# An attention and mixture-of-experts kernel: filler matmuls with a named bank, the expert loop's blocks in another order, and table reads taken ahead on ScalarE

## The chip, the cores and the metric

The kernel runs on one core of one Trainium2 chip. The metric is the device time of one execution, in microseconds (us). The kernel before took 606.84 us (median of three runs: 606.8, 606.84 and 608.63). The profile was taken in an execution of its own, which took 614.04 us.

## The reference

An attention without a score matrix feeds a layer of experts of which each token uses one.

```python
# q, k, v: 8 batches, 8 heads, 576 rows, 64 columns
q_s = softmax(q, axis=-1)                 # over the 64 columns
k_s = softmax(k, axis=2)                  # over the 576 rows
kv  = einsum('bhsd,bhse->bhde', k_s, v)   # 64 x 64 for each head
x   = einsum('bhsd,bhde->bhse', q_s, kv)  # turned to 4608 tokens x 512

logits = x @ w_gate                       # 8 experts
expert_idx = argmax(logits, axis=1)       # one expert for each token
gate_w = softmax(logits)[token, expert_idx]
for e in range(8):                        # tokens sorted by expert
    h = relu(x_sorted[lo:hi] @ w1[e])     # 512 -> 1024
    y_sorted[lo:hi] = h @ w2[e]           # 1024 -> 512
out = gate_w[:, None] * unsort(y_sorted)
```

## The kernel before

**Two stages.** The attention, the gate and the sorting of the tokens take about the first 199 us; they are straight code without a branch. Then comes a loop over blocks of tokens whose number and widths are known only at run time, since they depend on how many tokens went to each expert.

**The attention's order is written out by hand.** The string ORDER is a list of 804 words such as `TR.4.0.21`. A word names a step (TR), its batch (4) and its part (0). `Plan.emit` walks the list and lets each step issue its instructions on all the engines that it uses. So the place of a word in the list is the place of its instructions in the queue of each engine. Steps that matter below: KM0 to KM4 take the maximum of k, KS subtracts it, KE applies the exponential; QS and QE do the like for q; TR transposes a group of q (qT, L531, with the copy qTs by ScalarE, L536); KV forms the product of k and v (a matmul that sets the bank to a start value, L416, and the products, L427); G0, G2 transpose and gate with it (kvT, L451; kg, L460); MM multiplies q with kv (xp, L543 and L546); R0 to R9 and RB, RC, RD, RG rank the tokens of each expert (rk, L611 to L615, read on VectorE at L627).

**Fills.** A fourth number in a word is a count of fills: matmuls of a constant, 128 columns by 384, whose result nobody reads. They stand on TensorE ahead of the step's own instructions, in places where TensorE would sit idle, and keep it active. There are 215 of them, all issued at L220. A fill needs a PSUM bank to write to. `fill` asks `spots.oldest`, which looks at the live buffers of the pools tr, xp and sm and takes the one whose readers were issued longest ago; if there is none it takes the bank `hot`. The pool kv is not looked at. A fill that writes to a bank waits until the bank's readers are done, as every write does.

**The loop over blocks.** Each engine runs its own copy of a loop at run time, and the engines meet by semaphores. A table in SBUF (`tab`) holds a row of numbers for each pass: KD is the kind of the block, LW says that a new expert's weights begin. Kind 12 is a block of 3 x 128 tokens, 11, 10 and 9 are narrower by 32 tokens at a time, 3 to 8 have 2 x 128 tokens, and below 3 the block is tiny. TensorE's `body` reads the kind and branches: one of six pieces of code for layer 1 (`layer1`, 96 matmuls with their weight loads, L1009; or `tiny1`), and then layer 2, up to three times 24 matmuls (`layer2`, L1025, or `half`, L1067). The six pieces stand in the code one behind the other: tiny, 2 x 128, 288, 320, 352, and last 3 x 128. Behind them stands layer 2. In this case the passes have the kinds 12 (five times), 11, 8, 10, 8, 10, 8, 9, 8 and 2.

**The work around the loop's start.** Before the loop, TensorE finishes a layer 2 of the first block (L1107) and transposes the tokens of the next (L1123); ScalarE copies these to xh (L1154), VectorE makes the remainder xl (L1245), and the first layer 1 of the loop waits for xl. In the loop, ScalarE makes the high part of the hidden layer (`relus`, L1170) and VectorE the low part (L1259). VectorE's transposition of the next tokens (L1236) stands between the third and the fourth of the eight low parts, and waits for the loads xt and gx. ScalarE's `body` reads three numbers of the table at the start of a pass (kind, fresh, turn) and one more after the relus.

Of the kernel before, what the change touches and what calls it, by code (L numbers as in the profile page):

```python
# [37 lines left out]
LK.0.0 LK.0.1 LK.0.2 LV.0.0 LK.1.0 LK.1.1 LV.0.1 LV.0.2 LQ.0.0 LK.2.0 CD.0.0 LK.2.1 LV.1.0 LV.1.1 LV.1.2 KM0.0.0 KM0.0.1 KM1.0.0  # L38
KM2.0.0.24 KM3.0.0 KM4.0.0.4 KR.0.0 KS.0.1 KS.0.2 KS.0.0 KM0.1.0 KS.0.3 KM0.1.1 KM1.1.0 ER.0.0 KE.0.0 KE.0.2 KE.0.1 KE.0.3
KV.0.0.24 KM2.1.0.1 KV.0.1.1 KV.0.2.1 KV.0.3 KM3.1.0 N0.0.0 N1.0.0 QM.0.0 N2.0.0 G0.0.0.11 QS.0.0 G1.0.0 QE.0.0 QE.0.1 KM4.1.0  # L40
G2.0.0.16 TR.0.0 QS.0.1 KS.1.3 KS.1.2 KR.1.0 KS.1.0 KM0.2.0 KS.1.1 KM0.2.1 CS.0.0 KM1.2.0 QE.0.2 KE.1.3 ER.1.0 G3.0.0 QE.0.3
EX.0.0 TR.0.1.2 MM.0.0.1 TR.0.2 KE.1.2 KE.1.1 EX.0.1 EX.0.2 KE.1.0 KM2.2.0.1 TR.0.3 MM.0.1 KV.1.0 KV.1.1 KV.1.2.1 KV.1.3 LQ.1.0
WG.0.0 LQ.0.1 WG.0.1 LV.2.0 LQ.1.1 LV.2.1 LV.2.2 LK.3.0 LK.3.1 LV.3.0 WG.0.2 DE.0.0 RE.0.0 KM3.2.0 EV.0.0 DE.0.1 QM.1.0 RE.0.1
N0.1.0 N1.1.0 EV.0.1 WH.0.0 EX.0.3 N2.1.0 KM4.2.0 MM.0.2 MM.0.3.4 G0.1.0 KS.2.0 KS.2.3 DE.0.2 KR.2.0 QMR.1.0 KS.2.2 KS.2.1
RE.0.2 EV.0.2 DE.0.3 RE.0.3 EV.0.3 LS.0.0 QS.1.0 QS.1.1 QSR.1.0 WL.0.0 QE.1.0 KE.2.3 ER.2.0 QE.1.1 QE.1.2 KE.2.1 G1.1.0 WH.0.1
# [12 lines left out]
KM2.5.0 KV.4.1 KV.4.2 TR.3.4 MM.3.2 KV.4.3 KM0.6.0 R8.2.0 KM3.5.0 R6.1.0 RE.3.1 EV.3.1 KM0.6.1 N0.4.0 R1.2.0 DE.3.2 R3.2.0
N1.4.0 RE.3.2 R4.2.0 EV.3.2 QM.4.0 EX.3.4 N2.4.0 R9.2.0 MM.3.3 MM.3.4.3 KM4.5.0 R5.2.0 G0.4.0 RC.2.0 KS.5.1 DE.3.3 RG.2.0 KS.5.3
KR.5.0 KS.5.2 RB.2.0 RD.2.0 R6.2.0 KS.5.0 RE.3.3 KM1.6.0 EV.3.3 DE.3.4 PU.1.4 WL.0.3 WL.0.4 QS.4.0 QS.4.1 RH.2.0 PU.2.1 PU.2.0  # L60
TR.4.0.21 QE.4.0 ER.5.0 QE.4.1 G1.4.0 EX.4.0 TR.4.1 KM2.6.0.1 G2.4.0.1 RE.3.4 KM3.6.0 EV.3.4 LS.3.0 R0.3.0 R8.3.0 R1.3.0 R3.3.0
R4.3.0 QE.4.2 QE.4.3 KE.5.3 G3.4.0 KE.5.0 EX.4.1 KE.5.1 KE.5.2 R9.3.0 LQ.5.0 LQ.4.1 LV.6.0 LV.6.1 LV.6.2 LQ.5.1 WG.0.6 WG.0.7
LK.7.1 KV.5.0.3 MM.4.0 KM4.6.0 KV.5.1 KV.5.2 TR.4.2 R5.3.0 KV.5.3 MM.4.1 KR.6.0 DE.4.0 KS.6.2 KM0.7.0 RE.4.0 KS.6.1 RB.3.0
N0.5.0 RD.3.0 EV.4.0 RC.3.0 KS.6.0 N1.5.0 DE.4.1 RG.3.0 KS.6.3 R6.3.0 RE.4.1 QM.5.0 KM0.7.1 EV.4.1 QMR.5.0 KE.6.1 ER.6.0 N2.5.0
KE.6.0 WH.0.5 EX.4.2 KE.6.2 G0.5.0.17 TR.4.3.4 EX.4.3 G1.5.0 PU.2.3 RH.3.0 PU.2.2 PU.3.0 PU.3.2 QS.5.0 QSR.5.0 QS.5.1 KV.6.0
MM.4.2 KV.6.1 TR.5.0 MM.4.3 G2.5.0 KV.6.2 TR.5.1.1 QE.5.0 QE.5.1 QE.5.2 QE.5.3 KE.6.3 G3.5.0 WH.0.6 WH.0.7 EX.5.0 EX.5.1 LQ.6.0
LV.7.0 DE.4.2 RE.4.2 EV.4.2 DE.4.3 RE.4.3 KM1.7.0 EV.4.3 KV.6.3.1 MM.5.0 TR.5.2 MM.5.1 TR.5.3 EX.5.2 EX.5.3 LS.4.0 R0.4.0 N0.6.0
DE.5.0 N1.6.0 RE.5.0 R8.4.0 R1.4.0 EV.5.0 R3.4.0 R4.4.0 DE.5.1 QM.6.0 RE.5.1 TR.5.4 KM2.7.0 MM.5.2 R5.4.0 N2.6.0 R9.4.0 EX.5.4
PU.3.1 PU.3.3 PU.3.4 WL.0.6 RH.4.0 WL.0.5 WL.0.7 QS.6.0 QS.6.1 EV.5.1 KM3.7.0 DE.5.2 R6.4.0 RB.4.0 RE.5.2 RD.4.0 EV.5.2 G0.6.0.3
# [12 lines left out]
RB.7.3 VL.7.1 RD.7.3 L3.3.5 RH.7.3 RH.6.0 PU.6.2 PU.6.1 PU.6.0 RH.7.0 PU.6.3 PU.7.2 PU.7.4 PU.7.3 PU.7.1 PU.7.0 T3.7.0 L1.3.7
L1.3.6 L2.3.7 L2.3.6 T5.7.0 T6.7.0 L3.3.7 L3.3.6 T7.7.0 T8.7.0 L4.3.0 T9.7.0
# [5 lines left out]
class Spots:  # L89
    def __init__(self):  # L90
        self.last, self.of, self.count = {}, {}, 0

    def tile(self, pool, shape, *a, tag, **k):
        t = pool.tile(shape, *a, tag=tag, **k)
        if len(shape) == 3 and shape[1] == 2:
            self.last[tag] = t[:, 0, :HOT]
        elif len(shape) == 3 and shape[1] * shape[2] == 512:
            self.last[tag] = t[:, :HOT // shape[2], :]
        else:
            self.last[tag] = t[:, 512 - HOT:] if shape[1] == 512 and tag == "sm" else None  # L100
        return t

    def taken(self, tag, until, bufs):
        if tag in ("tr", "xp", "sm"):
            self.of[tag] = (self.of.get(tag, []) + [(self.last.get(tag), until)])[-bufs:]

    def oldest(self, when):
        best = None
        for tiles in self.of.values():
            for t, until in tiles:  # L110
                n = [when(a) for a in until]
                if t is not None and n and None not in n and (best is None or max(n) < best[0]):
                    best = max(n), t
        return best and best[1]


class Plan:
# [7 lines left out]
    def emit(self, order, fill):  # L125
# [5 lines left out]
        for key, word in zip(queue, words):  # L131
# [10 lines left out]
            if x.take:  # L142
                self.spots.taken(x.take, x.until, self.bufs[x.take])
# [804 lines left out]
def experts(nc, tc, g):  # L948
# [46 lines left out]
    def pe():  # L995
# [470 lines left out]
```

## Time and profile before

| what | value |
|---|---|
| median of three runs | 606.84 us |
| the profiled execution | 614.04 us |
| its span in the trace | 612.3 us |
| TensorE busy | 579.6 us, 95% of the span |
| VectorE busy | 315.4 us, 52% |
| ScalarE busy | 234.8 us, 38% |
| GpSimd busy | 131.0 us, 21% |
| loop's first matmul | at 217.83 us of the span |

The span runs from the first to the last instruction in the trace. The profiled execution was 7.2 us slower than the median of the runs. "PE" is TensorE, "PEld" its weight loads, "DVE" VectorE, "ACT" ScalarE, "POOL" GpSimd and "SP" the queue of SyncE, which here issues loads. A number in brackets at the end of a row is the time for which the engine had been idle, and the name behind the arrow is what ended that; "issue" means that the engine waited for nothing that the profile shows. [...]

### The profile page before, as it was taken

The page shows a single profiled execution, that of the slowest core. Times are in us where ns is not written, and L with a number is a line of the kernel's source. Part 1 is how long each engine was busy: PE and PEld are TensorE (multiplying, and loading weights), DVE is VectorE, ACT ScalarE, POOL GpSimd, SP SyncE. Part 2 cuts the span into 40 slices and gives each one's busy share as a digit, 9 for nine tenths or more (in the row PEclk, how much of TensorE's full clock was granted, in tenths as well). Part 3 has the DMA queues.
Part 4 walks back from the last instruction along what each step waited for, and adds up shares of the span by engine and source line. Part 5 has one row for each costly group of instructions (what it writes and reads, how often), then busy time and mean ns, then how long its engine had stood idle before and what let it go on. Part 6 is the DMA issues. An engine that isn't in the chain of part 4 may idle for free.

```text
span 612.3 us, 12035 instructions
## 1 busy us (share of the span) xinstructions
PE 579.6 (95%) x3870; PEld 505.8 (83%) x3871; DVE 315.4 (52%) x618; ACT 234.8 (38%) x492; POOL 131.0 (21%) x213
## 2 busy tenths in 40 slices
PE   8999997988998879999999999999999999999995
PEld 4677865766897679998989898989999898998983
DVE  5786898855785114062704141325561662466344
ACT  2564654645541212142512122224442552354244
POOL 3142474254516100102010101010101101010110
PEclk9999999989899979999999999999999999999998
DMA  9999989967158770308070302030634247054200
GB/s 246 277 272 297 265 247 251 265 208 215 61 204 307 228 209 20 85 0 240 3 220 17 86 17 52 34 70 22 202 108 131 45 161 220 12 173 154 72 17 22
DMA packets 88449, 87.81 MB, mean 143 GB/s; under 512 B 21855, under 2 KB 74591, under 8 KB 87776
## 3 DMA queue, kind: packets, MB, share of 16 engines
q1 hardware_dynamic: 82416, 67.18, 40.2%
q0 software_dynamic: 6000, 20.21, 9.0%
q8 instruction: 19, 0.31, 0.2%
q14 instruction: 14, 0.11, 0.1%
HBM read 63.88 MB, written 24.28 MB: 144 GB/s over the span
## 4 chain that ended last, share of the span: by engine, by line
PE 64%; issue 1%; DVE 1%; DMA 1%; ACT 0%; DVEq 0%; POOL 0%; SPq 0%; POOLq 0%
PE py L1025 29%; PE pt L1009 23%; PE ph L1009 8%; PE py L1107 1%; PE py L1067 1%; DMA xs<-xr,posi 1%; PE pt L1042 1%; DVE w2l L1250 0%; DVE xl L1245 0%; ACT xh L1154 0%; PE pt L1123 0%; PE ph L1033 0%; POOL out L1349 0%; PE pt L1052 0%; PE ph L1052 0%
## 5 line engine op out<-in xcount | busy, mean ns | idle before, releaser
L1025 PE MATMUL py<-w2h,hid 128*128 128x512 f32 x528 | 164.9, 389 | 0.0
L1259 DVE SCALAR_TENSOR_TENSOR hid<-pt,hid 128x384 fp32r<-128x384 f32 x78 | 42.8, 557 | 182.6 <-ACT hid L1170 175.2
L1025 PEld LDWEIGHTS py<-w2h,hid 128*128 128x128 f32 x528 | 99.1, 188 | 20.1
L1349 POOL DMA_INDIRECT out<-yt,ix x39 | 42.4, 1088 | 304.2 <-ACT yt L1139 289.6
L1025 PE MATMUL py<-w2l,hid 128*128 128x512 f32 x264 | 102.7, 389 | 0.0
L1139 ACT ACTIVATE yt<-py,ga 128x512 f32<-128x512 f32 x36 | 24.7, 687 | 132.1 <-PE py L1025 117.9
L1170 ACT ACTIVATE hid<-pt 128x384 fp32r<-128x384 f32 x78 | 38.3, 492 | 96.0 <-PE pt L1009 78.6
L1009 PE MATMUL pt<-xh,w1h 128*128 128x384 f32 (+4 forms) x312 | 60.4, 316 | 5.3 <-issue 5.3
L1009 PE MATMUL pt<-xh,w1l 128*128 128x384 f32 (+4 forms) x312 | 59.9, 314 | 0.0
L1009 PE MATMUL pt<-xl,w1h 128*128 128x384 f32 (+4 forms) x312 | 59.9, 314 | 0.0
L1025 PEld LDWEIGHTS py<-w2l,hid 128*128 128x128 f32 x264 | 49.6, 188 | 9.8
L1009 PEld LDWEIGHTS pt<-xh,w1h 128*128 128x128 f32 x312 | 51.2, 192 | 6.7 <-issue 5.7
L1009 PEld LDWEIGHTS pt<-xl,w1h 128*128 128x128 f32 x312 | 50.3, 191 | 0.0
L1009 PEld LDWEIGHTS pt<-xh,w1l 128*128 128x128 f32 x312 | 50.3, 191 | 0.0
L645 POOL DMA_INDIRECT xs<-xr,posi x36 | 37.6, 1044 | 30.7 <-DVE xr L637 19.9
L543 PE MATMUL xp<-kx,qTs 128*128 128x146 f32 x256 | 40.0, 302 | 1.3 <-DVE xr L558 0.7
L1236 DVE STREAM_TRANSPOSE xrow<-xt 128x1536 f32<-128x1536 f32 x13 | 38.6, 2972 | 1.0 <-DMA gx<-xs 1.0
L543 PEld LDWEIGHTS xp<-kx,qTs 128*128 128x128 f32 x256 | 35.4, 199 | 3.6 <-issue 2.6
L220 PEld LDWEIGHTS <-ones 128*128 128x128 bf16 x215 | 21.6, 103 | 20.1 <-issue 8.5
L493 POOL TENSOR_TENSOR qs<-qt,qm 128x1024 f32<-128x1024 f32 (+1 forms) x16 | 23.8, 1500 | 66.7 <-DVE qm L488 35.5
L427 PE MATMUL kv<-vt,kt 128*64 128x65 f32 (+1 forms) x640 | 31.9, 237 | 1.7 <-issue 1.5
L427 PEld LDWEIGHTS kv<-vt,kt 128*64 128x64 f32 (+1 forms) x640 | 25.2, 141 | 9.7 <-issue 5.5
(245 smaller groups left out, 864.6 us busy)
## 6 DMA issues: line engine op xcount, KB each, us to landing
raw<-in_moe_w SPq DMA_DIRECT2D x10, 2048.0 KB, 9.7
vt<-in_v SPq DMA_DIRECT2D x16, 512.0 KB
qt<-in_q SPq DMA_DIRECT2D x8, 1024.0 KB
kt<-in_k SPq DMA_DIRECT2D x7, 1024.0 KB
xt<-xs SPq DMA_DIRECT2D x32, 192.0 KB
xs<-zr SPq DMA_DIRECT2D x11, 292.0 KB
xt<-in_moe_w SPq DMA_DIRECT2D x8, 256.0 KB
raw<-in_moe_w SPq DMA_DIRECT2D x4, 512.0 KB
```

Of the source, the lines that this page charges most:

```text
L220: nc.tensor.matmul(hot.t if to is None else to, ones16, ones16[:, None, :].to_broadcast([P, HOT // P, P]), start=True, stop=True)
L427: nc.tensor.matmul(o.kv[i * D:(i + 1) * D, c, lo:lo + D + 1], o.kt[:r, 2 * c + i, j, :], VT[b % 2][:r, 2 * c + i, at:at + D + 1], start=Fa ...
L493: nc.gpsimd.tensor_tensor(o.qs[:, j0:j1].rearrange("p j h d -> p h j d"), o.qt[:, :, j0:j1, :], o.qm[:, :, j0:j1, None].to_broadcast([P, H ...
L543: nc.tensor.matmul(xv[:, c, :KW], o.qT[i][:, c, :], kx[:, c, :], start=True, stop=True)
L645: s = nc.gpsimd.indirect_dma_start(out=xs, out_offset=bass.IndirectOffsetOnAxis(ap=n.pi[:, t - t0:t - t0 + 1], axis=0), in_=xr[:, t, :], i ...
L1009: m = e.matmul(ph, wt[:, c, f * P:(f + 1) * P], xt[:, c, :w], start=(n == 0), stop=(n == 3 * NC - 1))
L1025: m = e.matmul(g.PY[u], ht[:, f, u * P:(u + 1) * P], wt[:, f, :], start=(n == 0), stop=(n == 3 * NF - 1))
L1139: m = e.activation(g.YT[u], g.PY[u], AF.Copy, scale=g.GA[:, u:u + 1]).wait_op(sPY[u], cu[u], GE)
L1170: e.activation(g.HH[:, f, :], g.PH[f][:, :W], AF.Relu).wait_op(sPH[f], it, GE).then_inc(sHH[f], 1)
L1236: e.transpose(g.XR.rearrange("p c (k j) -> p k c j", j=32), xblocks(g.XT).rearrange("p k (l c) -> p k c l", c=NC)).wait_op(sX, ld, GE).the ...
L1259: e.scalar_tensor_tensor(g.HL[:, f, :], g.PH[f][:, :W], 0.0, g.HH[:, f, :].bitcast(F32), op0=ALU.max, op1=ALU.subtract).wait_op(sHH[f], it ...
L1349: e.indirect_dma_start(out=g.out, out_offset=bass.IndirectOffsetOnAxis(ap=g.IX[:, u:u + 1], axis=0), in_=g.YT[u], in_offset=None, bounds_c ...
```

## The change

**Fills.** A word now names the bank too: `TR.4.0.30.KV-4-0` puts 30 fills into the buffer that the step KV.4.0 took. `fill` looks the buffer up; `oldest` is gone. The buffers of the pool kv are now among those that can be named. Into such a buffer a fill writes 256 columns instead of 384, and most counts were raised to match. There are 250 fills instead of 215, with 80,256 columns instead of 82,560. The order of all other steps is as it was.

```diff
-TR.4.0.21 QE.4.0 ER.5.0 QE.4.1 G1.4.0 EX.4.0 TR.4.1 KM2.6.0.1 G2.4.0.1 RE.3.4 KM3.6.0 EV.3.4 LS.3.0 R0.3.0 R8.3.0 R1.3.0 R3.3.0
...
+RB.2.0 RD.2.0 R6.2.0 KS.5.0 RE.3.3 KM1.6.0 EV.3.3 DE.3.4 PU.1.4 WL.0.3 WL.0.4 QS.4.0 QS.4.1 RH.2.0 PU.2.1 PU.2.0 TR.4.0.30.KV-4-0
+QE.4.0 ER.5.0 QE.4.1 G1.4.0 EX.4.0 TR.4.1 KM2.6.0.1.KV-4-0 G2.4.0.1.KV-4-0 RE.3.4 KM3.6.0 EV.3.4 LS.3.0 R0.3.0 R8.3.0 R1.3.0
...
-    def fill(n):
-        to = spots.oldest(plan.when) if n else None
-        for _ in range(n):
-            nc.tensor.matmul(hot.t if to is None else to, ones16, ones16[:, None, :].to_broadcast([P, HOT // P, P]), start=True, stop=True)
+    def fill(n=0, key=None):
+        to = spots.of[key] if key else hot.t
+        for _ in range(int(n)):
+            nc.tensor.matmul(to, ones16, ones16[:, None, :].to_broadcast([P, 2 if key and key[:2] == "KV" else HOT // P, P]), start=True, stop=True)
```

On TensorE this is what stands before, behind the transpositions kvT of step G0.4 (rk is the bank of the ranks of the tokens, ones_109 the constant):

```order
L615 MATMUL rk<-oh_131,ones_109 128x8
L451 MATMUL kvT<-ident,kx_98 128x128 [waits Activation_49] x4
L220 LDWEIGHTS ones_109
L220 MATMUL rk<-ones_109 128x384 [waits DVE_49]
...
L531 MATMUL qT<-ident,qs 128x128 [waits Activation_49,Pool_49]
...
L384 MATMUL kmT<-ident,km 128x128 [waits DVE_49,Activation_49]
...
L460 MATMUL kg<-wg,kvTs 128x16 [waits PE_49]
```

And this is the same place after, where line numbers are lower by 6:

```order
L609 MATMUL rk<-oh_131,ones_109 128x8
L445 MATMUL kvT<-ident,kx_98 128x128 [waits Activation_49] x4
L214 LDWEIGHTS ones_109
L214 MATMUL kv<-ones_109 128x256
...
L525 MATMUL qT<-ident,qs 128x128 [waits Activation_49,Pool_49]
...
L378 MATMUL kmT<-ident,km 128x128 [waits DVE_49,Activation_49]
...
L454 MATMUL kg<-wg,kvTs 128x16 x4
...
L410 MATMUL kv<-eps_111,ones_109 128x264 [waits PE_49]
```

The fills ahead of the transpositions qT no longer wait for VectorE; the matmul that starts the next kv now waits for TensorE's own fills in that bank.

**The loop on TensorE.** The piece for 3 x 128 tokens now stands first, the tiny one last.

```diff
         def body(j):
             kind = x.get(KD, j, 0, 12)
-            with e.If(kind < 9):
-                with e.If(kind < 3):
-                    tiny1()
-                with e.If(kind > 2):
-                    layer1(2 * P)
-            with e.If(kind > 8):
-                with e.If(kind < 12):
+            with e.If(kind > 11):
+                layer1(3 * P)
+            with e.If(kind < 12):
+                with e.If(kind > 8):
+                    with e.If(kind > 10):
+                        layer1(11 * Q)
                     with e.If(kind < 11):
+                        with e.If(kind > 9):
+                            layer1(10 * Q)
                         with e.If(kind < 10):
                             layer1(9 * Q)
-                        with e.If(kind > 9):
-                            layer1(10 * Q)
-                    with e.If(kind > 10):
-                        layer1(11 * Q)
-                with e.If(kind > 11):
-                    layer1(3 * P)
+                with e.If(kind < 9):
+                    with e.If(kind > 2):
+                        layer1(2 * P)
+                    with e.If(kind < 3):
+                        tiny1()
```

Of the loop on TensorE before, from the read of the kind to the start of layer 2, these are the first branch, the first matmuls of two of the six pieces (the last number of a row is the piece's width: 256 and 384 tokens), and the first branch and matmul of layer 2:

```order
L985 TENSOR_LOAD tab
L985 ISA x2
L1079 COMPARE_AND_BRANCH
...
L1009 MATMUL pt<-xh,w1h_61 128x256 [waits sw10,sxl]
...
L1009 MATMUL pt<-xh,w1h_61 128x384 [waits sw10,sxl]
...
L1096 COMPARE_AND_BRANCH
L982 REGISTER_ALU [waits syt0]
L1025 MATMUL py<-w2h_2240,hid 128x512 [waits sw20,shl0]
```

After, the same stretch (L1036 is the tiny piece):

```order
L979 TENSOR_LOAD tab
L979 ISA x2
L1073 COMPARE_AND_BRANCH
L1003 MATMUL pt<-xh,w1h_61 128x384 [waits sw10,sxl]
...
L1003 MATMUL pt<-xh,w1h_61 128x256 [waits sw10,sxl]
...
L1036 MATMUL pt<-w1h_61,xh 128x512 [waits sw11,sw10,sxl]
...
L1090 COMPARE_AND_BRANCH
L976 REGISTER_ALU [waits syt0]
L1019 MATMUL py<-w2h_2275,hid 128x512 [waits sw20,shl0]
```

For kind 12, five pieces lay between the read of the kind and layer 1, and none between layer 1 and layer 2; now it is the other way round.

**The loop on ScalarE.** The kind and the flag of a pass are kept in two registers and copied there at the end of the pass before; the first pair is read ahead of the loop.

```diff
         def body(j):
-            kind = x.get(KD, j, 0, 12)
-            fresh = x.get(LW, j, 0, 1)
-            turn = x.get(LW, j + 1, 0, 1)
+            kind = e.snap(kd, min_val=0, max_val=12)
+            fresh = e.snap(lw, min_val=0, max_val=1)
             for run in (tiny, relus):
...
             x.add("it", 1)
-            with e.If(x.get(KD, j + 1, 0, 12) > 0):
+            more = x.get(KD, j + 1, 0, 12)
+            turn = x.get(LW, j + 1, 0, 1)
+            with e.If(more > 0):
                 evac()
...
+            e.reg_mov(kd, more)
+            e.reg_mov(lw, turn)
```

## Rows read from the trace of the kernel before

**Rows 1.** Page, groups: busy, mean ns; idle before.

```profile
L1025 PE MATMUL py<-w2h,hid 128*128 128x512 f32 x528 | 164.9, 389 | 0.0
L1009 PE MATMUL pt<-xh,w1h 128*128 128x384 f32 (+4 forms) x312 | 60.4, 316 | 5.3 <-issue 5.3
```

**Rows 2.** Chain that ended last, from 205 us: start, us, what.

```profile
213.09 4.74 issue
217.83 8.67 PE pt L1009 x36
226.50 4.16 PE ph L1009 x24
230.66 6.24 PE pt L1009 x36
236.91 16.33 PE py L1025 x72
```

**Rows 3.** Windows, all engines: stretch, length, busy of each; PEclk, DMA share, GB/s.

```profile
95.00:122.00 27.00, 22.73 (x236) 17.18 (x235) 22.25 (x50) 15.48 (x45) 11.67 (x17) 1.00 0.96 250
130.40:133.90 3.50, 3.50 (x37) 2.94 (x36) 0.17 (x1) 0.60 (x1) 2.44 (x3) 0.51 1.05 372
150.90:157.80 6.90, 6.90 (x46) 6.20 (x46) 3.19 (x12) 2.91 (x11) 0.00 (x0) 0.51 0.21 76
200.00:213.00 13.00, 12.56 (x61) 10.26 (x59) 1.68 (x2) 3.23 (x4) 2.00 (x2) 1.00 0.75 231
215.80:222.60 6.80, 4.77 (x15) 4.80 (x16) 0.03 (x1) 0.56 (x2) 0.19 (x1) 0.50 1.07 323
```

**Rows 4.** DMA queues, 205 to 217 us: packets, MB, share of 16 engines.

```profile
q8 instruction: 3, 0.05, 2.2%
```

**Rows 5.** DMA queues, 246 to 612 us (all that there are).

```profile
q1 hardware_dynamic: 23943, 24.30, 23.7%
q0 software_dynamic: 2880, 8.65, 6.5%
```

**Rows 6.** Waits of TensorE: total us, times, longest.

```profile
PE qT L220 <- ACT qTs L536: 0.8, 1, 0.8
PE mb L220 <- DVE kt L409: 0.5, 1, 0.5
```

**Rows 7.** Timeline of TensorE, 97 to 107 us: start, us, row [idle before].

```profile
97.58 0.64 PE L451 MATMUL kvT<-ident,kx 128*128 128x128 f32 x4
100.73 3.57 PE L220 MATMUL rk<-ones 128*128 128x384 bf16 x21 [2.51 <-DVE rs L627]
104.14 1.04 PE L531 MATMUL qT<-ident,qs 128*128 128x128 f32 x8
105.99 0.33 PE L220 MATMUL rk<-ones 128*128 128x384 bf16 x1
106.37 1.06 PE L460 MATMUL kg<-wg,kvTs 128*128 128x16 f32 x8
```

**Rows 8.** Timelines of GpSimd and ScalarE: a source of that qT, and its reader.

```profile
98.10 2.93 POOL L493 TENSOR_TENSOR qs<-qt,qm 128x1024 f32<-128x1024 f32 x2 [7.58 <-DVE own L630]
104.84 0.60 ACT L536 ACTIVATE qTs<-qT 128x512 f32<-128x512 f32 x1 [3.09 <-issue]
```

**Rows 9.** Timeline of TensorE, other short stops, and the last matmul ahead of the loop.

```profile
129.65 0.66 PE L531 MATMUL qT<-ident,qs 128*128 128x128 f32 x4 [1.84 <-remote]
150.45 0.84 PE L427 MATMUL kv<-vt,kt 128*64 128x65 f32 x11 [1.08 <-issue]
199.59 0.59 PE L1114 MATMUL ph<-ones 128*128 128x512 bf16 x2 [2.02 <-SPq L927]
212.18 0.39 PE L1107 MATMUL py<-w2h,hid 128*128 128x512 f32 x1
```

**Rows 10.** Timeline of VectorE, first pass of the loop.

```profile
228.58 2.93 DVE L1236 STREAM_TRANSPOSE xrow<-xt 128x1536 f32<-128x1536 f32 x1 [0.96 <-DMA gx<-xs]
```

**Rows 11.** Timeline of ScalarE, start of the last pass.

```profile
596.96 0.63 ACT L1163 ACTIVATE w2h<-raw 128x512 fp32r<-128x512 f32 x1 [2.23 <-issue]
```

More of the change, by code (lines that the diff above doesn't have):

```diff
@@ L42 @@
[L42 to L45, printed above, removed]
@@ new lines @@
+N2.1.0 KM4.2.0 MM.0.2 MM.0.3.4.G2-0-0 G0.1.0 KS.2.0 KS.2.3 DE.0.2 KR.2.0 QMR.1.0 KS.2.2 KS.2.1 RE.0.2 EV.0.2 DE.0.3 RE.0.3
+EV.0.3 LS.0.0 QS.1.0 QS.1.1 QSR.1.0 WL.0.0 QE.1.0 KE.2.3 ER.2.0 QE.1.1 QE.1.2 KE.2.1 G1.1.0 WH.0.1 KE.2.0 QE.1.3
+TR.1.0.8.G2-0-0 G2.1.0.3.G2-0-0 TR.1.1 KV.2.0.1.KV-1-0 KV.2.1.1.MM-0-2 EX.1.0 KE.2.2 G3.1.0 EX.1.1 KV.2.2 TR.1.2 MM.1.0 MM.1.1
+KV.2.3 TR.1.3 LQ.2.0 LV.3.1 WG.0.3 LK.4.0 LV.3.2 LK.5.0 LK.4.1 R0.0.0 R8.0.0 KM0.3.0 R1.0.0 KM0.3.1 R3.0.0 DE.1.0 RE.1.0 N0.2.0
+N1.2.0 EV.1.0 KM1.3.0 DE.1.1 RE.1.1 R4.0.0 EV.1.1 R9.0.0 N2.2.0 EX.1.2 EX.1.3 G0.2.0.12.G2-1-0 TR.1.4 R5.0.0 MM.1.2 MM.1.3
@@ new lines @@
+KV.3.3.1.G2-2-0 MM.2.1 TR.2.3 KM2.4.0 LS.1.0 R0.1.0 DE.2.0 RE.2.0 N0.3.0 N1.3.0 R8.1.0 EV.2.0 R1.1.0 DE.2.1 RE.2.1 KM3.4.0
+R3.1.0 EV.2.1 R6.0.0 R4.1.0 N2.3.0 EX.2.3 MM.2.2 G0.3.0.1.G2-2-0 MM.2.3 KM4.4.0 R5.1.0 R9.1.0 G1.3.0 WH.0.4 RC.1.0 QM.3.0
+DE.2.2 KS.4.0 RG.1.0 RE.2.2 RB.1.0 KS.4.2 RD.1.0 QMR.3.0 KR.4.0 EV.2.2 KS.4.1 DE.2.3 RE.2.3 KS.4.3 EV.2.3 KM0.5.0 KM0.5.1
+RH.1.0 WL.0.2 QS.3.0 PU.1.0 QSR.3.0 PU.1.2 PU.1.3 PU.1.1 QS.3.1 TR.3.0.35.KV-3-0 TR.3.1 G2.3.0 QE.3.0 ER.4.0 QE.3.1 WH.0.3
+KE.4.0 G3.3.0 EX.3.0 QE.3.2 QE.3.3 EX.3.1 KE.4.1 KE.4.2 TR.3.2.7.KV-3-0 MM.3.0 KV.4.0 TR.3.3 MM.3.1 LQ.4.0 LV.5.0 LV.5.1 WG.0.5
@@ L84 @@
+T2.7.0 L1.3.4 R5.7.3 L1.3.5 PD.7.0 VH.7.1 L2.3.4 L2.3.5 RG.7.3 RC.7.0 VL.7.3 RG.7.0 L3.3.4 RB.7.3 VL.7.1 RD.7.3 L3.3.5 RH.7.3
+RH.6.0 PU.6.2 PU.6.1 PU.6.0 RH.7.0 PU.6.3 PU.7.2 PU.7.4 PU.7.3 PU.7.1 PU.7.0 T3.7.0 L1.3.7 L1.3.6 L2.3.7 L2.3.6 T5.7.0 T6.7.0
+L3.3.7 L3.3.6 T7.7.0 T8.7.0 L4.3.0 T9.7.0
 """
@@ L90, in __init__ @@
     def __init__(self):
-        self.last, self.of, self.count = {}, {}, 0
+        self.last, self.of = {}, {}
     def tile(self, pool, shape, *a, tag, **k):
         t = pool.tile(shape, *a, tag=tag, **k)
-        if len(shape) == 3 and shape[1] == 2:
+        if tag == "kv":
+            self.last[tag] = t.rearrange("p a b -> p (a b)")[:, :256] if len(shape) == 3 else None
+        elif len(shape) == 3 and shape[1] == 2:
             self.last[tag] = t[:, 0, :HOT]
@@ L99, in tile, with taken @@
         else:
-            self.last[tag] = t[:, 512 - HOT:] if shape[1] == 512 and tag == "sm" else None
+            self.last[tag] = t[:, 512 - HOT:] if shape[1] == 512 else None
         return t
[L103 to L114, printed above, removed]
+    def taken(self, key, tag):
+        self.of["-".join(map(str, key))] = self.last.get(tag)
 class Plan:
@@ L128, in emit @@
         assert sorted(queue) == sorted(self.steps)
-        seen = {}
+        seen = set()
         taken = {t: [] for t in self.bufs}
@@ L137, in emit @@
                 taken[x.take].append(x)
-            self.when = lambda a: seen.get(a, -1 if a not in self.steps else None)
-            fill(int(word[3]) if len(word) > 3 else 0)
-            seen[key] = len(seen)
+            seen.add(key)
+            fill(*word[3:])
             x.fn()
             if x.take:
-                self.spots.taken(x.take, x.until, self.bufs[x.take])
+                self.spots.taken(key, x.take)
 @with_exitstack
@@ L743, in first_l2 @@
     def first_l2():
-        py = I0.py = kvs.tile([P, DM], F32, name="py", tag="kv")
+        py = I0.py = spots.tile(kvs, [P, DM], F32, name="py", tag="kv")
         n = 0
@@ L1224, in act @@
         yout(2, again=False)
+        kd, lw = x.reg("kd", x.get(KD, 0, 0, 12)), x.reg("lw", x.get(LW, 0, 0, 1))
         x.walk(body)
```

78 lines of the change are left out of this document (36 added, 42 removed).

## The prediction

> **What bounds the kernel now.** I read the page's groups first. TensorE is busy for 95% of the span, and its matmuls in the loop follow one another without a stop: L1025 shows an idle time of 0.0 before 528 matmuls, and L1009 shows 5.3 us, all put down to "issue" [rows 1]. The waits of TensorE say how often an idle time occurs; that of L1009 is one. So in the loop a change can gain on TensorE by doing less work, by a higher clock, or by removing this one stop; nothing in the change makes the work less.
>
> The chain tells where the stop is: the last thing that the first layer 1 of the loop needs, VectorE's xl, ends at 213.09, and layer 1 starts only at 217.83, and the 4.74 us between are "issue" [rows 2]. In the code nothing lies there but the entry to the loop, the read of the kind and the branches to the piece for 3 x 128 tokens, which stands behind five others. In the 12 us around it the queue that fetches instructions moved 3 packets, 0.05 MB [rows 4]; in the 366 us behind 246 us it does not appear at all [rows 5], though every pass jumps through the same code. I read the stop as code that isn't on the engine yet when the branch asks for it, and that is there in all later passes.
>
> The chain shows a second cost: the first 36 matmuls took 8.67 us, the same number later 6.24 us [rows 2]. [...]
>
> In the attention I read the waits of TensorE ahead of fills, of which rows 6 show two lesser ones, and then the timeline around the longest. The kvT transpositions end at 98.22, the 21 fills that follow start at 100.73, since the bank rk is read by VectorE until then, and step TR.4.0 starts behind them at 104.14 [rows 7]. Its data from GpSimd were there at 101.03, and ScalarE, which copies its result, had been idle for 3.09 us when it came [rows 8]. These fills thus delayed the work that they were to bridge.
>
> **The change part by part.**
>
> *Fills at TR.4.0.* The bank kv has no reader left there, so the wait of 2.51 us goes. The fills are 30 x 256 = 7,680 columns in place of 21 x 384 = 8,064; at 3.57 us for the latter that is 3.40, so 0.17 less. They would run from 98.22 to 101.62, behind GpSimd's 101.03, so that nothing else is late for this step: TR.4.0 starts about 2.68 us earlier.
>
> *Other fills.* The waits of fills for qTs (0.8) and kt (0.5) go too [rows 6], 1.3 together, if what follows them is not late for the same reason. Against this, seven of the eight matmuls that start a kv now wait for TensorE's own fills, one did before. What such a wait costs is seen at kg, which waits for TensorE itself: the fill before it ends at 106.32 and kg starts at 106.37 [rows 7], while qT, which does not wait for it, starts at 104.14, 0.16 us ahead of the end of the fills in front of it at 104.30 [rows 7]. So 0.21 us each, 6 x 0.21 = 1.26 us at most. Behind it are queued kv's products, which need kt anyway. I count the two as -1.3 and +1.2.
>
> *What of this reaches the end.* The attention gains 2.68 + 1.3 - 1.2 = 2.8 us on TensorE. Not all need arrive: the DMA share is 0.96 from 95 to 122 us [rows 3], so loads may be late where matmuls now come earlier. I bound the part from below at 1.0 us (a third) and from above at 2.68 + 1.3 = 4.0, and take 2.8, since what TR.4.0 waited for was no load.
>
> *Entry to the loop.* The piece for 3 x 128 now stands right behind the read of the kind, so the jump over five pieces is gone. Of the 4.74 us nothing remains but the table read and the two branches, and of the clock's loss 8.67 - 6.24 = 2.43 us goes, as TensorE would stop for only 0.5 us, from 212.57 [rows 9] to 213.09. Layer 1 would start at 213.15 and end 6.24 + 4.16 + 6.24 = 16.64 us later, at 229.79. Layer 2 started at 236.91; the gain up to here is 7.1 us.
>
> *Is layer 2 ready then?* VectorE's transposition L1236 waited for gx and ended at 231.51 [rows 10]; the fourth low part comes behind it. Layer 2 needs the fourth after nine matmuls of 16.33/72 = 0.227 us, 2.04 us, so from 229.5 on it may begin with a loss of no more than that part's own time. That is level with 229.79, and I leave the gain at 7.1.
>
> *The jump goes to another place.* The five pieces now lie between the 3 x 128 piece and layer 2. The first pass must jump over them for the first time there. Nothing in the trace shows a first jump behind matmuls. From above, the nearest row is the old jump: 4.74 us. From below, the jumps of later passes: 0.0 at L1025 [rows 1]. The truth should lie between, because the branch is taken by the engine's sequencer while matmuls it has issued are still running, and because the weight loads that fill the DMA engines (share 1.07 at 215.8 to 222.6 [rows 3]) are further along by then. I take 2.0 us, a bit under the middle.
>
> [...]
>
> *The clock behind that stop.* A stop of about 2 us may or may not cost clock. Behind stops of 1.84 us (before 129.65) and 1.08 (before 150.45) [rows 9] the clock was 0.51 for 3.5 and 6.9 us; behind 2.51 (before 100.73) and 2.02 (before 199.59) it stayed at 1.00 [rows 3, 7, 9]. So half the time 1.7 to 3.4 us; I put in half of 2.4, 1.2 us.
>
> *ScalarE.* Its reads of the table leave the start of a pass. They show in the last pass, as 2.23 us of "issue" before 596.96 [rows 11]. That is the upper bound; the lower is 0, since TensorE has layer 1's matmuls beside it, and its list of waits has none for ScalarE in the loop above 0.2 us. I take 0.1. The reads now stand before xh, which the next layer 1 needs only after 16 us of layer 2.
>
> *Sum.* Against the profiled execution (614.04 us): -2.8 attention, -7.1 entry, +2.0 new stop, +1.2 clock, -0.1 ScalarE = -6.8, or 607.2. That execution was 7.2 us slower than the median of the runs, and I can't tell which of its stops the others share; the stops before 129.65 and 150.45 may be among its own. The places that I count are waits for code and banks, which do not depend on chance, so I apply the sum to the median: 606.84 - 6.8 = 600.0 us.
>
> **The rivals.**
>
> A. The jump to layer 2 is wholly hidden behind the matmuls. For it: all later passes. Against it: a first jump has cost 4.74. Then 606.84 - 2.8 - 7.1 = 596.9; with the upper bound of the attention 606.84 - 4.0 - 7.1 = 595.7.
>
> B. The stop only moves: layer 2 waits 4.74 us and the clock falls behind it (2.43), which eats the 7.1 of the entry, and of the attention 1 to 2.8 us arrive. For it: the same five pieces are jumped over. Against it: the DMA engines are less busy there. Then 606.84 less 1 to 2.8 is 604.0 to 605.8.
>
> C. The fills do nothing for the end, because loads set the pace until 122 us (share 0.96), while the loop gains 4.0. Then 602.8. Against it: ScalarE stood idle for TR.4.0, not for a load [rows 8].
>
> D. Slower. The jump over five pieces is paid in each of the five passes with 3 x 128 tokens, where before, the way from layer 1 to layer 2 was straight. It decides from (7.1 + 2.8) / 5 = 2.0 us a pass on; at 4.74 it makes +23.7, so 606.84 - 9.9 + 23.7 = 620.6. Against it: before, these passes jumped over the same pieces at their start and returned from the end of the code, all without a stop [rows 1], and no instruction packets are seen after 246 us [rows 5]. [...]
>
> **How the numbers follow.** My forecast 0.47, A 0.25, B 0.13, C 0.10, D 0.05. The range from 595.7 (A with all of the attention) to 604.8 (near the middle of B) leaves out D and half of B and the far end of A. No change that can be told means within 0.3%, 1.8 us, so from 605.0 to 608.7: a part of B and the tail of C, 0.08. Slower: D, 0.05. Faster 0.87.
>
> **What would show it.** Right: the first matmul of the loop within 0.5 us of xl's end; the clock 1.00 over the first 36 matmuls and these 6.24 us; a stop of 0 to 4.7 us before the first py of the first pass, with instruction packets just before it; the fills of TR.4.0 begin at once behind kvT, and ScalarE's wait for it shrinks by about 2.5 us. Wrong: a stop at the head of later 3 x 128 layer 2 with instruction packets in each pass (D); the first layer 1 still late though nothing is jumped over (then the stop was not the jump, but the loop's entry or its table read); the gain at 104 us gone again by 199 (C).

## The result

The changed kernel took 598.17 us (median of four runs, 597.81 to 599.03) beside 607.74 for the kernel before on the same chips: a ratio of 0.9843, 95% interval [0.9817, 0.9869]. On another chip the ratio was 0.982 [0.9772, 0.9867]. The forecast was 600.0 us with a range of 595.7 to 604.8. The profiled execution took 598.51 us, its span is 596.7, and TensorE is busy for 571.4 us of it.

The chain of the changed kernel around the loop's start (columns as in [rows 2]), where L1243 is xl, L1003 layer 1 and L1019 layer 2:

```profile
200.12 1.77 DVE xl L1243
201.89 0.04 issue
201.94 6.51 PE pt L1003 x36
208.45 4.16 PE ph L1003 x24
212.61 6.24 PE pt L1003 x36
218.85 0.74 issue
219.60 16.60 PE py L1019 x72
```

The 4.74 us of "issue" in [rows 2] are 0.04, the first 36 matmuls take 6.51 us in place of 8.67, and a new stop of 0.74 us stands before the first layer 2, where the branch over the five pieces (L1075) takes 3.6 us by the trace's record of it, from 215.59 to 219.18 us, which the views leave out. From xl to layer 2 it takes 17.7 us where it took 23.8. Further on, the chain has a second new stop, in the first block of 320 tokens:

```profile
368.09 5.28 PE pt L1003 x36
373.37 3.52 PE ph L1003 x24
376.89 5.28 PE pt L1003 x36
382.17 1.36 issue
383.53 11.14 PE py L1019 x48
```

The chain also corrects the list of kinds given ahead: five passes of 384 tokens are followed by 320, 256, 352, 256, 352, 256, 288, 256 and the tiny one, that is 12 (five times), 10, 8, 11, 8, 11, 8, 9, 8, 2.

The windows of the changed kernel over both places (columns as in [rows 3], where PEclk is the clock that TensorE was granted, as a share of full speed), and the row of the instruction queue from 246 to 590 us:

```profile
95.00:122.00 27.00, 24.29 (x270) 19.69 (x271) 23.51 (x52) 16.85 (x49) 13.48 (x19) 1.00 0.98 245
202.00:219.00 17.00, 16.85 (x96) 16.53 (x96) 5.35 (x6) 3.74 (x10) 1.17 (x2) 1.00 0.74 207
219.00:240.00 21.00, 20.40 (x95) 17.59 (x96) 3.96 (x7) 4.52 (x7) 2.94 (x3) 1.00 0.33 78
366.00:384.00 18.00, 16.64 (x108) 16.00 (x107) 7.55 (x10) 5.14 (x11) 1.17 (x2) 1.00 0.07 27
```

```profile
q8 instruction: 4, 0.07, 0.1%
```

The clock stays at 1.00 through both new stops. And where the kernel before has no instruction packet behind 246 us [rows 5], the changed one has four (0.07 MB), all of them around the first block of 320 tokens: at 367.2, 380.5, 383.9 and 387.0 us.

In the attention, TensorE's timeline, and then ScalarE's row for TR.4.0, answer to [rows 7, 8]:

```profile
96.81 0.64 PE L445 MATMUL kvT<-ident,kx 128*128 128x128 f32 x4
97.28 3.44 PE L214 MATMUL kv<-ones 128*128 128x256 bf16 x30
101.11 1.06 PE L525 MATMUL qT<-ident,qs 128*128 128x128 f32 x8 [0.39 <-ACT kvTs L449]
```

```profile
101.84 0.60 ACT L530 ACTIVATE qTs<-qT 128x512 f32<-128x512 f32 x1 [0.87 <-PE qT L525]
```

The fills start at once and take 3.44 us (3.40 forecast). The next thing late is ScalarE's kvTs, the copy of kvT, by 0.39 us. ScalarE's stop is 0.87 us in place of 3.09.

### The profile page after: what moved, and what is told of

It reads as the page before. It is cut to its first block, busy times and chain, and to the rows that moved or that the text cites. A ratio compares the mean times of both kernels' runs of the same rounds, so it can differ in the third digit from the quotient of the medians.

```text
span 596.7 us, 12019 instructions
## 1 busy us (share of the span) xinstructions
PE 571.4 (96%) x3905; PEld 502.3 (84%) x3906; DVE 317.6 (53%) x618; ACT 235.9 (40%) x492; POOL 132.1 (22%) x213
## 4 chain that ended last, share of the span: by engine, by line
PE 66%; issue 1%; DVE 1%; DMA 1%; ACT 0%; DVEq 0%; POOL 0%; SPq 0%; POOLq 0%
PE py L1019 30%; PE pt L1003 24%; PE ph L1003 8%; PE py L1101 1%; PE py L1061 1%; PE pt L1036 1%; DMA xs<-xr,posi 1%; DVE w2l L1248 0%; DVE xl L1243 0%; ACT xh L1148 0%; PE pt L1117 0%; PE ph L1027 0%; POOL out L1347 0%; PE ph L1046 0%; PE pt L1046 0%
## 5 line engine op out<-in xcount | busy, mean ns | idle before, releaser
L1019 PE MATMUL py<-w2h,hid 128*128 128x512 f32 x528 | 165.0, 390 | 2.1 <-issue 2.1
L1019 PEld LDWEIGHTS py<-w2h,hid 128*128 128x128 f32 x528 | 99.1, 188 | 22.8 <-issue 2.6
L1019 PE MATMUL py<-w2l,hid 128*128 128x512 f32 x264 | 102.7, 389 | 0.0
L1003 PE MATMUL pt<-xh,w1h 128*128 128x384 f32 (+4 forms) x312 | 59.4, 312 | 0.6 <-DVE xl L1243 0.6
L1003 PE MATMUL pt<-xh,w1l 128*128 128x384 f32 (+4 forms) x312 | 59.3, 312 | 0.0
L1003 PE MATMUL pt<-xl,w1h 128*128 128x384 f32 (+4 forms) x312 | 59.3, 312 | 0.0
L1019 PEld LDWEIGHTS py<-w2l,hid 128*128 128x128 f32 x264 | 49.6, 188 | 9.8
L1003 PEld LDWEIGHTS pt<-xh,w1h 128*128 128x128 f32 x312 | 50.2, 189 | 2.0 <-DVE xl L1243 1.0
L1003 PEld LDWEIGHTS pt<-xh,w1l 128*128 128x128 f32 x312 | 49.8, 189 | 0.0
L1003 PEld LDWEIGHTS pt<-xl,w1h 128*128 128x128 f32 x312 | 49.8, 189 | 0.0
L537 PE MATMUL xp<-kx,qTs 128*128 128x146 f32 x256 | 38.3, 293 | 1.4 <-DVE xr L552 0.6
L487 POOL TENSOR_TENSOR qs<-qt,qm 128x1024 f32<-128x1024 f32 (+1 forms) x16 | 23.8, 1500 | 60.4 <-DVE qm L482 27.0
L537 PEld LDWEIGHTS xp<-kx,qTs 128*128 128x128 f32 x256 | 33.6, 190 | 3.4 <-issue 1.7
L214 PEld LDWEIGHTS <-ones 128*128 128x128 bf16 x250 | 24.8, 101 | 12.0 <-issue 3.0
L421 PEld LDWEIGHTS kv<-vt,kt 128*64 128x64 f32 (+1 forms) x640 | 23.9, 136 | 9.5 <-issue 3.6
L421 PE MATMUL kv<-vt,kt 128*64 128x65 f32 (+1 forms) x640 | 30.3, 231 | 1.3 <-DMA vt<-in_v 1.2
```

What stands on the lines that cost most here:

```text
L214: nc.tensor.matmul(to, ones16, ones16[:, None, :].to_broadcast([P, 2 if key and key[:2] == "KV" else HOT // P, P]), start=True, stop=True)
L421: nc.tensor.matmul(o.kv[i * D:(i + 1) * D, c, lo:lo + D + 1], o.kt[:r, 2 * c + i, j, :], VT[b % 2][:r, 2 * c + i, at:at + D + 1], start=Fa ...
L487: nc.gpsimd.tensor_tensor(o.qs[:, j0:j1].rearrange("p j h d -> p h j d"), o.qt[:, :, j0:j1, :], o.qm[:, :, j0:j1, None].to_broadcast([P, H ...
L537: nc.tensor.matmul(xv[:, c, :KW], o.qT[i][:, c, :], kx[:, c, :], start=True, stop=True)
L1003: m = e.matmul(ph, wt[:, c, f * P:(f + 1) * P], xt[:, c, :w], start=(n == 0), stop=(n == 3 * NC - 1))
L1019: m = e.matmul(g.PY[u], ht[:, f, u * P:(u + 1) * P], wt[:, f, :], start=(n == 0), stop=(n == 3 * NF - 1))
```

## The experiments

Each took the kernel before or the changed one and altered one thing; each was timed beside the kernel before.

**One part alone: the order of the pieces.** The kernel before with the new `body` of TensorE.

> The kernel before with only the new order of the pieces of layer 1 on TensorE. Theory (the loop's gain is the old entry jump, less two first jumps behind layer 1): the profile of the changed kernel has 17.7 us from xl's end to layer 2 in place of 23.8, and loses 1.4 + 0.3 us later in the block of 320 tokens and in the first layer 2; so -4.5 us, with the first matmul of the loop within 0.6 us of xl. Rival (the stop at the entry came from the state of the loads in that one profiled run, not from the jump): within 1 us of the kernel before.

603.05 us beside 606.94, ratio 0.9921 [0.9897, 0.9945], -4.8 us (-4.5 expected). Layer 1 follows xl by 0.04 us, a stop of 0.81 stands before layer 2, and one of 1.48 behind layer 1 of the first block of 320:

```profile
206.42 0.04 issue
206.46 6.54 PE pt L1009 x36
223.40 0.81 issue
```

The loop's gain is the jump's, as the theory has it.

**One part alone: ScalarE's registers.** The kernel before with `kd` and `lw`.

> The kernel before with only ScalarE's table reads taken ahead. Theory: -0.1 us, below what can be told; the stop at the loop's entry is there. Rival (ScalarE's reads delay the end of the kernel by their whole 2.2 us): -2 us, with the last pass shorter. This run also gives a second profile of the attention of before: if the stops before 129.65 and 150.45 us are its own, they come again; if they are chance, they don't.

607.66 beside 606.94, ratio 1.0 [0.9986, 1.0014]: nothing. Its profile (606.74 us, span 604.9) is the better picture of the kernel before, and is called the clean profile below: the stops before 129.65 and 150.45 in [rows 9] are not in it. Its chain, with L1249 as xl:

```profile
204.01 1.77 DVE xl L1249
205.78 5.47 issue
211.25 7.99 PE pt L1009 x36
219.23 4.16 PE ph L1009 x24
223.39 6.24 PE pt L1009 x36
229.63 16.33 PE py L1025 x72
```

xl ends at 205.8 here, at 213.1 in the profile read for the prediction. So the 7 us between that execution and the median were lost in the attention, in stops and stretches at a clock of 0.51 [rows 3, 9] that this execution does not have, and the attention's gain is 205.78 - 201.89 = 3.9 us, not the 11.2 that the two first profiles show side by side. Other profiles agree: with the old fills xl ends at 205.6 to 206.4 us in three of them, with all the new fills at 201.0 to 202.7 in eight; the two profiles with stops like those of [rows 9] are left aside. From xl to layer 2 it is 23.85 us, as before. Two rows of its timeline, against which TR.4.0 is read below:

```profile
97.38 0.64 PE L451 MATMUL kvT<-ident,kx 128*128 128x128 f32 x4
103.94 1.04 PE L531 MATMUL qT<-ident,qs 128*128 128x128 f32 x8
```

**One part alone: the fills.**

> The kernel before with only the new fills (banks and counts); loop code as before. Theory (a held-up bank delays TR.4.0 and a few others, the rest is small): -2.8 us by the prediction's sum; what is left of the measured 9.6 after the loop's 4.5 would be -5. Rival (loads set the pace of the attention, fills give nothing): within 1 us. The 4.7 us stop at the loop's entry must still be there.

606.3 beside 606.94, ratio 0.9983 [0.9966, 1.0]: -1.0 us, a fifth of the 5 that were left to explain. But xl is earlier by 4.3 us (201.4), and all of it is lost between xl and layer 2, as its chain shows:

```profile
199.68 1.77 DVE xl L1239
201.44 5.00 issue
206.44 4.50 PE pt L1003 x13
210.94 1.97 issue
212.91 7.02 PE pt L1003 x23
219.93 4.16 PE ph L1003 x24
224.09 6.24 PE pt L1003 x36
230.33 16.33 PE py L1019 x72
```

28.9 us instead of 23.85: a second stop of 1.97 us after 13 matmuls of layer 1, with an instruction packet on record from 209.9 to 211.3 us, and a clock of 0.50 from 206 to 215 us in its windows. (This execution took 607.46 us, 1.2 more than the median.) The new fills put 74 more instructions in front of the loop (35 weight loads, 35 matmuls, 4 waits), and I suspected that the second stop comes from the place where the loop's code now lies.

**The fills with the loop's code in another place.**

```diff
         count = x.count()
+        with e.If(count < 2):
+            ones(90)
```

> The kernel with only the new fills, and ahead of the loop on TensorE 182 instructions that a branch always skips, so that the loop's code lies 256 instructions behind where it lay before, instead of 74. [...]

603.3 beside 608.27, ratio 0.9923 [0.9906, 0.9941], -4.7 us (some 602.7 was expected if the place of the code made the second stop, some 606 if not). Its chain has one stop again and 36 matmuls in one piece:

```profile
199.27 1.77 DVE xl L1241
201.04 6.53 issue
207.57 8.11 PE pt L1003 x36
```

From xl to layer 2 it is 25.05 us. So 182 instructions that never run give back most of what the fills alone had lost: by the ratios 0.9983 - 0.9923 = 0.006 or 3.6 us. The fills are the same in both runs, so I put the difference down to the place of the code; why one place has the second stop and the other not, the traces don't show. The first stop became longer, 6.53 in place of 5.00: the late branch has a record of 8.1 us in place of 7.25, and the one ahead of it 1.2 in place of 0.4. The branch over the 182 instructions is not in it; it took 0.4 us at 190.2, 11 us before.

**The first jump without the weights beside it.** The kernel before, with SyncE's first load of the next expert's weights held back.

```diff
+        e.wait_ge(sGS, 1)
         with e.If(x.get(LIVE, 1, 0, 1) > 0):
             wload(x.get(EO, 1, 0, E - 1), False)
```

> The kernel before, with the first load of the next expert's weights held back until the first block's gs is there (about when xl ends). Theory (the first jump takes so long, 7 us from the branch, because its fetch shares the DMA engines with 4 MB of weights; the first jumps behind layer 1 took 3.4 to 3.6 us without them): the stop at the loop's entry falls from 5 us to 1.5 to 2.5 us and the clock stays up, so -3 to -4.5 us. Rival (the fetch takes its time whatever the load): the stop stays at 4.7 to 5.5 us, time within 1 us of before.

606.9 beside 608.27, ratio 0.9981 [0.9967, 0.9995]. TensorE's idle time at the entry falls from 5.99 us (in the clean profile) to 3.19, as its timeline shows; the trace's record of the late branch itself shrinks from 7.7 to 4.9 us. The clock does not stay up: it is 0.84 from 208 to 219 us, and the first 36 matmuls take 7.92 us (208.29 to 216.21) where the same number later takes 6.24. And of the 2.9 us gained from xl to layer 2, 1.9 are lost within layer 2, which waits for a low part of VectorE, and that for gx, now behind the late weights:

```profile
208.29 1.13 PE L1009 MATMUL pt<-xh,w1h 128*128 128x384 f32 x4 [3.19 <-issue]
```

```profile
226.89 2.90 DVE L1236 STREAM_TRANSPOSE xrow<-xt 128x1536 f32<-128x1536 f32 x1 [9.40 <-DMA gx<-xs]
```

So with the weights beside it the late branch's record is longer, by some 2.8 us in the clean profile (by 2.1 in the first one, whose record is 7.0); that the time would fall by 3 us was wrong (it fell by 1), as the loads mostly changed places.

**TR.4.0 back in the bank of the ranks.** The changed kernel with one word altered: `TR.4.0.30.KV-4-0` to `TR.4.0.21.R5-2-0`.

> The changed kernel with the fills of TR.4.0 back in the bank of the ranks, 21 of 384 columns. Theory (this place carries 2.7 of the attention's gain of about 4): +2.5 to +2.8 us on the changed kernel, some 600.8, with the wait of 2.5 us for VectorE back. Rival (the gain comes from many places, and what is late here is caught up by 199 us): within 1 us of the changed kernel. The loop's code lies 27 instructions earlier than in the changed kernel, which can move its two stops by some tenths.

601.46 beside 608.27, ratio 0.9894 [0.9877, 0.991], where the changed kernel had 0.9843 and 0.982: 3.1 to 4.5 us more by the medians and ratios, where 2.5 to 2.8 were expected. Its profile, taken in the fastest of its executions (600.11 us), has 2.0 us more at xl's end (203.95 for 201.94 at the first layer 1) and 1.6 in the span. Its timeline has the old wait:

```profile
100.19 3.57 PE L214 MATMUL rk<-ones 128*128 128x384 bf16 x21 [2.52 <-DVE rs L621]
```

By this, the place carries half of the attention's 3.9 us or more.

**The piece of 320 next to layer 2.** The changed kernel, with the order 384, 256, tiny, 352, 288, 320.

```diff
             with e.If(kind < 12):
+                with e.If(kind < 9):
+                    with e.If(kind > 2):
+                        layer1(2 * P)
+                    with e.If(kind < 3):
+                        tiny1()
                 with e.If(kind > 8):
                     with e.If(kind > 10):
                         layer1(11 * Q)
                     with e.If(kind < 11):
-                        with e.If(kind > 9):
-                            layer1(10 * Q)
                         with e.If(kind < 10):
                             layer1(9 * Q)
-                with e.If(kind < 9):
-                    with e.If(kind > 2):
-                        layer1(2 * P)
-                    with e.If(kind < 3):
-                        tiny1()
+                        with e.If(kind > 9):
+                            layer1(10 * Q)
```

> The changed kernel with the pieces in the order 384, 256, tiny, 352, 288, 320, so that the piece for 320 tokens is next to layer 2. Theory (each first jump to code that is not there costs 3.4 us of the sequencer, which TensorE feels only as far as queued matmuls don't cover it): the stop of 1.36 us behind the block of 320 goes, that of 0.74 in the first pass stays; -1.4 us on the changed kernel if no other first jump is late, 0 if the stop only moves to the next block of 256 or 352.

600.08 beside 608.27, ratio 0.9864 [0.9843, 0.9886]: no gain, rather a loss. The stop behind layer 1 of the block of 320 went, and one of 2.08 us stands at its front, with a clock of 0.80 over the 8.4 us from its start:

```profile
369.77 0.82 PE L1003 MATMUL pt<-xh,w1h 128*128 128x320 f32 x4 [2.08 <-issue]
```

```profile
367.60:376.00 8.40, 6.13 (x31) 5.67 (x31) 0.64 (x2) 1.76 (x4) 1.16 (x2) 0.80 0.10 35
```

The records of the late branches are alike (2.9 to 3.7 us behind layer 1 in five profiles, 3.2 here). What differs is the lead, the time for which matmuls already queued still run when the late branch begins: 3.3 and 2.4 us at the two stops of the changed kernel, 1.9 here. At the head of a pass, the branch back and the read of the table stand in the code between the last matmul and the late branch; that they use up a part of the lead is my estimate from these numbers.

**Fewer pieces.** The changed kernel with the pieces 384, 256 and tiny only.

> The changed kernel with only three pieces of layer 1: 384 for every block wider than 256, 256, and tiny; the results are the same, TensorE does more: one block of 320, two of 352 and one of 288 at 384, 2.56 + 2 x 1.28 + 4.0 = 9.1 us more. Theory (distance makes the stops): no stop or one under 0.4 us before layer 2 in the first pass and none at the first narrower block, so about 7 us above the changed kernel. Rival (the first jump over pieces is late however many they are): both stops there, about 9 us above.

605.31 us in one run, beside 608.47. Its chain goes from layer 1 to layer 2 without a stop, in the first pass and in all later ones, and no late branch is on record (the longest of the loop's branches took 0.5 us):

```profile
212.97 6.24 PE pt L1003 x36
219.21 16.33 PE py L1019 x72
```

So the first jump over the pieces for 256 tokens and tiny alone is not late here, as the theory had it; the 9.1 us of added matmuls less 2.4 of stops are 6.7, near the 7.4 above 597.9. How long a single jump is does not decide by itself: in the changed kernel's block of 320 the late branch (L1084, 3.4 us) is a jump over these same two pieces, right behind a jump over the piece for 288. And in the kernel before, the "jump over five pieces" was two: that over the tiny piece and the one for 256 took 0.5 us, and only that over 288, 320 and 352 behind it (L1085) was late, by 7.0 us. The records fit a target too far beyond the code that has run, but that is only a reading; no run shows how far is too far, or why.

**The wide pieces behind layer 2.**

```diff
-            with e.If(kind > 11):
+            with e.If(kind + e.snap(up, min_val=0, max_val=3) > 11):
                 layer1(3 * P)
...
             x.add("it", 1)
+            e.reg_mov(x.r["up"], 0)
+            then = x.get(KD, j + 1, 0, 12)
+            with e.If(then < 12):
...
```

> The changed kernel with the pieces for 352, 320 and 288 tokens moved behind layer 2, to the end of a pass, where they do layer 1 of the next block if it is so wide; a first block of such a width is done at 384. Between the piece for 384 and layer 2 only those for 256 tokens and the tiny one are left. [...] Rival (any first jump costs the same wherever it leads, as when the block of 320 stood last): 0 to +1.5 us.

(`up` is 3 in the first pass and 0 from then on; this does a wide first block at 384.) 599.8 beside 608.47, ratio 0.9846 [0.9798, 0.9895]: not the gain of 1 to 2 us on the changed kernel that was expected. Both stops are gone (the first jump over the pieces for 256 and tiny takes 0.5 us), but the first jump over the wide pieces, at the end of the first pass (record 4.1 us), costs more than both:

```profile
219.70 16.32 PE py L1019 x72
236.02 2.82 issue
238.84 8.06 PE pt L1003 x36
```

**The kind read ahead on TensorE too.** In the last kernel, `then` is read ahead of layer 2 and kept in a register for the next pass.

> The kernel with the wide pieces behind layer 2, in which TensorE also reads the next block's kind ahead of layer 2 and keeps it in a register, as ScalarE does. Theory (the 2.82 us stop at the end of the first pass is a late jump of 4.1 us less what matmuls are still queued, and the two table reads around it use up that lead): about 1 us less stop, and if the clock stays up behind it 1.8 us more, so 1 to 3 us below the kernel without it (599.8), at best 1 us below the changed kernel. Rival (the stop is the fetch alone): no change against 599.8.

603.17 beside 615.3, ratio 0.9806 [0.9783, 0.983]. The stop at the end of the first pass is 0.83 us. This profile has stops of 1.9 us ("remote") and 1.1 ("issue") in the attention, like those in [rows 9]; the kernel before was not profiled on this chip, but its time is near the 614.04 of that execution.

> The kernel with the wide pieces behind layer 2 and the kind read ahead, once more on another chip; on the one where it ran, both it and the kernel before stopped twice in the attention for reasons of that chip. Theory (its loop takes 393.3 us from xl's end to the end of the span, the changed kernel's 394.5 to 394.8): 1.3 us below the changed kernel, a ratio of 0.980 to 0.982 to before, with one stop of about 0.8 us in the loop. Rival (the new order of pieces only moved the stops): a ratio of 0.984 or more.

596.69 beside 607.54, ratio 0.9818 [0.9798, 0.9838]. The stop is 0.66 us, where the kernel without the read ahead had 2.82, and the clock stays up (36 matmuls in 6.48 us in place of 8.06); the late branch takes 3.4 us in place of 4.1, and the lead is 3.6 in place of 2.9:

```profile
218.76 16.32 PE py L1019 x72
235.08 0.66 issue
235.74 6.48 PE pt L1003 x36
```

From xl's end to the end of the span it is 594.9 - 201.8 = 393.1 us, against 596.7 - 201.9 = 394.8 and 597.0 - 202.5 = 394.5 in two profiles of the changed kernel. The profiles show one stop in place of two, and some 1.5 us less. But the intervals of the ratios overlap, and the second ratio of the changed kernel (below) is 0.982 too: that this kernel is the faster one is not shown.

**The changed kernel once more.**

> The changed kernel once more, beside the others on this chip: 0.984 of before by the first comparison. It gives a second profile: stops of 0.7 and 1.4 us before layer 2 of the first block and of the first block of 320 if they belong to the program, others if they are chance.

597.9 beside 608.47, ratio 0.982 [0.9772, 0.9867]. The stops before layer 2 are 0.62 and 1.15 us, at the same two places: they belong to the program.

## Why the prediction was right, and where it was not

*Fills at TR.4.0: right.* 2.68 us were forecast; against the clean profile TensorE's qT comes 2.3 us earlier beyond what was gained up to there (kvT by 0.57 us, 97.38 to 96.81; qT by 2.83, 103.94 to 101.11), and undoing this one word costs 2.0 us at the loop's start and 3 us or more in the medians. What is late next was not nothing, as I wrote, but ScalarE's kvTs by 0.39 us.

*Other fills: sized too low.* I had them at 1.3 gained and 1.2 lost. By the two profiles they gave 3.9 - 2.3 = 1.6 us: 0.6 up to 97 us, and 1.0 behind 104, where 0.9 was lost again between 118 and 124 us. No experiment took these places one by one. The waits of a starting kv for the fills in its bank, 1.2 in the sum, do not show: the idle time ahead of that matmul is 0.2 us in all, as before. In all the attention gave 3.9 us, 2.8 forecast, inside the bounds of 1.0 and 4.0. Loads were late here and there (waits for vt of 1.2 us in all in the changed kernel's list, 0.3 in the clean profile), not as much as rival C needs.

*Entry to the loop: right.* 7.1 us were forecast, 4.74 of stop and 2.43 of clock, less 0.06 of stop that stays; that the 2.43 are the clock's is read from the 0.50 granted from 215.8 to 222.6 us [rows 3]. Against the clean profile, stop and lost clock were 5.47 + 1.75 = 7.2, of which 0.3 remain: 6.9 gained.

*The jump that moved: right in kind, wrong in place and size.* 2.0 us were taken for the first pass, between 0 and 4.74. It is 0.6 to 0.8, since the matmuls queued ahead cover 3.3 us, most of the branch's 3.6. But I had counted one jump, and there is a second: in the first block of 320 tokens, 1.0 to 1.5 us in four profiles. I had argued from [rows 5] that after the first passes all code is there. The kernel before has no packet behind 246 us; in the changed kernel there is one at 367.2 us, just ahead of the first block of 320, and the jump from it to layer 2 was late again (3.4 us), though layer 2 had run five times. With 0.3 us in the first layer 2, the three sum to 2.4, where 2.0 for one stop and 1.2 for the clock were put in: that the sum is near is luck.

*Clock behind the stop: wrong.* I put in 1.2 us; it stayed at 1.00 behind both stops. A stop of 2.08 us and one of 2.82 in the experiments did cost clock (0.80 over 8.4 us; 36 matmuls in 8.06 us in place of 6.24), one of 1.36 did not; but of the stops in the attention 1.08 and 1.84 did and 2.02 and 2.51 did not [rows 3, 7, 9], so the length alone does not tell.

*ScalarE: right.* Nothing alone; in the last pass, its stop of 2.23 us [rows 11] is 0.53, and the time from that pass's first matmul to the end of the span went from 18.3 to 18.1 us.

*Rival D* did not happen: passes two to five go on without a stop, and between 246 and 367 us there is no instruction packet. The late first jumps in the loop have records of 2.9 to 4.1 us each.

The sum was -6.8 us; the medians moved by -8.7 from 606.84 and by -9.6 from 607.74. Against the clean profile the ledger closes: -3.9 attention, -6.1 from xl to layer 2 and +1.8 behind it (most of it the second stop and the slower first layer 2) is -8.2 us in the spans (604.9 to 596.7). What the first profile could not tell is that parts are not simply added: the fills alone gave 1 us and the order alone 4.8, together 9, because in the old order the place of the loop's code, moved by the fills' own instructions, cost most of what the fills had gained: with 182 skipped instructions ahead of the loop, the same fills gave 4.7.

## What to carry to other kernels

Filler work must go to a buffer that is free at that moment in time, and not to the one whose readers were issued longest ago: here one such choice made TensorE wait 2.5 us, and the step behind it came 2.3 us later than with a free bank. A long first jump over code that has not run yet was late here (three pieces or more; two, straight from running code, took 0.5 us). At five stops in the loop, with records of 3.2 to 4.1 us and leads of 1.9 to 3.6, TensorE stood still for 0.4 to 1.6 us more than the record less the lead: for 0.66 us behind the longest lead, and for 2.08 behind the shortest. With 4 MB of weights loading beside the jump its record was 7.7 us, and 4.9 without. So put such a jump where the queue is long and no big load runs, and read the loop's table early. Before believing a timing of one part alone, look whether its added instructions moved the code of a loop: 74 instructions cost 5 us here in the profile, and 182 that never run gave most of it back.

## What the runs showed of the hardware that was not expected

A late branch took 2.9 to 3.7 us by the trace's records behind a layer 1 in the loop, 3.2 to 4.1 at the head or the end of a pass, 4.9 at the entry with the weights held back, and 7.0 to 8.1 with 4 MB of weights loading beside it. That it waits for code that isn't there is a reading: instruction packets stand beside it, 3 of them (0.05 MB) at the entry [rows 4], and in the changed kernel one at 216.6 us, within the record that runs from 215.59 to 219.18, and one at 380.5, within that from 379.78 to 383.13.

In the changed kernel the jump to layer 2 was late in the first block of 320 tokens, though layer 2 had run in five passes, the last four without an instruction packet. Of the four packets (0.07 MB), one came just ahead of the block, one during the late branch and two behind it, and none after, though the pieces for 256, 352 and 288 tokens and the tiny one had still to run for the first time. What the packets brought, no run here can tell. In the kernel with three pieces and in those with the wide pieces behind layer 2, no packet is seen behind 246 us.

And of two executions of the same kernel (the one with the kind read ahead, on two chips) one had stops of 1.9 us ("remote") and 1.1 us ("issue") in the attention, with a clock of 0.94 from 100 to 190 us, that the other had not; its clock was 0.999 over the whole execution.
